# Loading the weights of two modes at a time: doubled places and doubled loads from mode 17 to mode 46 of a spectral-mix kernel

## Chip, cores, metric

One core of one Trainium2 chip. The metric is the device time of one execution in microseconds (us); the medians are over repeated runs. The span of a profile is a little shorter than the device time (424.8 us against 426.6 us for the kernel before), as it runs from the first to the last instruction of the program. An execution in which the core's clock is held lower would be set apart as slow.

## The reference

A sliding-window causal attention over 8 batches, 8 heads, 576 positions of 64 channels gives x of shape 8 x 576 x 512. Then follows a spectral mix, which is where the change lies:

```python
X = np.fft.rfft(x, axis=1)                       # along the sequence
Xr, Xi = np.real(X[:, :64]), np.imag(X[:, :64])  # 64 modes are kept
Yr = einsum('bmd,mde->bme', Xr, w_r) - einsum('bmd,mde->bme', Xi, w_i)
Yi = einsum('bmd,mde->bme', Xr, w_i) + einsum('bmd,mde->bme', Xi, w_r)
...                                              # inverse transform, y
u = x + y
return u + np.maximum(u @ w_ch, 0.0)
```

Each of the 64 modes has its own 512 x 512 matrices w_r and w_i in fp32, 1 MiB each. Mode 0 needs only w_r, so 127 matrices are read, each once: 133 MB of the 162.5 MB that the kernel reads. The arithmetic per matrix is small (8 batches), so this is a kernel that streams weights.

## The kernel before

It has three phases: attention (to about 147 us), the modes (to 390 us), and a tail that turns the modes back and writes the output. Weights are narrowed from fp32 to bf16 by the DMA, which only GpSimd (POOL) issues here, and start in the attention phase. Every load fills one place of 512 KB:

```python
def load_w(i, pool, tag, wt=None):
    m, im = divmod(i + (i > 0), 2)             # mode, real or imaginary
    if wt is None:
        wt = pool.tile([128, NC, DM], BF16, name="wt", tag=tag)
    src = moe_w_i if im else moe_w_r
    nc.gpsimd.dma_start(out=wt, in_=src[m].rearrange("(p c) e -> p c e", c=NC))
    wtiles[m, im] = wt
```

33 loads (modes 0 to 16) go out during the attention phase. From then on a place is refilled as soon as its mode has been used. There are 13 such places: LW = 5 that last to the end ("wl") and MW = 8 that are later needed for other data ("wm", which may hold no mode from 48, 50, 52 or 54 on). One more and then three more are opened late.

```python
def refill_w(m, im):                           # after the matmuls of (m, im)
    nonlocal nw
    i = max(2 * m - 1 + im, 0)
    if i in slot_of:
        free.append(slot_of.pop(i))
    if im or not m:
        free.extend(opens.pop(m, []))
    while nw < NLOAD and free:
        kind, j, last = slot = free.pop(0)
        if mode_of(nw) >= last:
            continue
        ...                                    # load_w into that place
        slot_of[nw] = slot
        nw += 1
```

A mode is eight matmuls on TensorE (PE), four on w_r and four on w_i, with other work between the modes. In the cuts of code, three dots mark what is left out, and the comments after # are mine.

The softmax here doesn't subtract the row's maximum and nothing guards it: scores larger than these inputs give would overflow.

Of the kernel before, what the change touches and what calls it, by code (L numbers as in the profile page):

```python
# [10 lines left out]
FP32R = mybir.dt.float32r  # L11
BF16 = mybir.dt.bfloat16
# [8 lines left out]
def view(ap, off, dims):  # L21

    return bass.AP(ap.tensor, ap.offset + off, [list(ap.ap[0])] + [list(d) for d in dims])
# [3 lines left out]
def kernel(  # L27
# [10 lines left out]
    nc = tc.nc  # L38
    B, H, S, D = q.shape
    NM = moe_w_r.shape[0]  # L40
    DM = moe_w_ch.shape[0]
# [4 lines left out]
    NC = DM // 128  # L46
    VW = 66
    RUN = S // 32
    LW = 5
    EW = 13  # L50
# [12 lines left out]
    keep = ctx.enter_context(tc.tile_pool(name="keep", bufs=1))  # L63
    wl = ExitStack()
    xqp = wl.enter_context(tc.tile_pool(name="xqp", bufs=1))
    wlate = wl.enter_context(tc.tile_pool(name="wlate", bufs=LW))

    ident_bf = consts.tile([128, 128], BF16, name="ident_bf")
    ident_r = consts.tile([128, 128], FP32R, name="ident_r")
    x_sb = keep.tile([128, B, NT, DM], BF16, name="x_sb")  # L70
    XQ = xqp.tile([128, NC, 3, B, NM], BF16, name="XQ")


    p1 = ExitStack()
    wearly = p1.enter_context(tc.tile_pool(name="wearly", bufs=EW, side="right"))
# [28 lines left out]
    NLOAD = 2 * NM - 1  # L104
    wtiles = {}

    def mode_of(i):
        return (i + 1) // 2

    def load_w(i, pool, tag, wt=None):  # L110
        m, im = divmod(i + (i > 0), 2)
        if wt is None:
            wt = pool.tile([128, NC, DM], BF16, name="wt", tag=tag)
        src = moe_w_i if im else moe_w_r
        nc.gpsimd.dma_start(out=wt, in_=src[m].rearrange("(p c) e -> p c e", c=NC))  # L115
        wtiles[m, im] = wt

    trigF = acons.tile([128, NT, 2 * NM], BF16, name="trigF")
    warm = acons.tile([128, 512], BF16, name="warm")
# [223 lines left out]
    def dft_turn(b):  # L343
        ps = ps_misc.tile([128, NC, 2, NM], BF16, name="pxq", tag="misc")
        for c in range(NC):
            nc.tensor.transpose(out=ps[:, c, :, :].rearrange("p r m -> p (r m)"), in_=Xs[b][:, c, :],
                                identity=ident_bf)
        nc.vector.tensor_copy(out=view(XQ, (B + b) * NM, [[3 * B * NM, NC], [B * NM, 2], [1, NM]]), in_=ps)
        nc.scalar.mul(out=view(XQ, b * NM, [[3 * B * NM, NC], [1, NM]]), in_=ps[:, :, 1, :], mul=-1.0)

    nw = 0
    EARLY = LW + EW

    def early(n):
        nonlocal nw
        for _ in range(n):
            if nw < EARLY:
                pool, tag = (wlate, "wl") if nw < LW else (wearly, "we")
                load_w(nw, pool, tag)
                nw += 1  # L360

    def spare(t):
# [28 lines left out]
    with tc.manual_schedule(engines={mybir.EngineType.PE, mybir.EngineType.Pool}):  # L391
# [49 lines left out]
        for w in range(last_unit + 1, NWIN + 1):  # L441
# [14 lines left out]
            if w in (NWIN - 4, NWIN - 1):  # L456
                i = (B - 2) % 2 if w == NWIN - 4 else (B - 1) % 2
                spare(kTs[i])
                spare(qtp.tile([128, 4, S], BF16, name="qT"))
            if w in (NWIN - 4, NWIN):  # L460
                i = (B - 2) % 2 if w == NWIN - 4 else (B - 1) % 2
                for j in range(2):
                    spare(vts[i][:, j])
                if w == NWIN - 4:
                    vt_mode = mode_of(nw - 1)
# [23 lines left out]
    YTl = late.tile([128, NC, B, R], FP32R, name="YTl")  # L489
    wch = late.tile([128, NC, DM], FP32R, name="wch")  # L490

    MW = 8
    wmid = p2.enter_context(tc.tile_pool(name="wmid", bufs=1, side="right", reuse_waits="tile"))
    mids = {j: wmid.tile([128, NC, DM], BF16, name="wt", tag=f"wm{j}") for j in range(MW)}
    late2 = p2.enter_context(tc.tile_pool(name="late2", bufs=1, side="right", reuse_waits="tile"))

    trigI = late2.tile([128, S + 128], FP32R, name="trigI")
# [7 lines left out]
    M0 = L0 * MG  # L505
# [2 lines left out]
    ML = MG - NLM  # L508
    ME = NM - NLM
    slot_of, opens = {}, {}  # L510
    for j in range(LW):
        opens.setdefault(mode_of(j), []).append(("wl", j, NM))
    for j in range(MW):
        at = mode_of(LW + (j > 1) * (EW + 1 - j)) if j else vt_mode
        opens.setdefault(at, []).append(("wm", j, M0 + 2 * (j // 2)))
    free = []

    def refill_w(m, im):

        nonlocal nw  # L520
        i = max(2 * m - 1 + im, 0)
        if i in slot_of:
            free.append(slot_of.pop(i))
        if im or not m:
            free.extend(opens.pop(m, []))
        while nw < NLOAD and free:
            kind, j, last = slot = free.pop(0)
            if mode_of(nw) >= last:
                continue
            if kind == "wl":  # L530
                load_w(nw, wlate, "wl")
            elif kind == "wx":
                load_w(nw, wx, "wx")
            elif kind == "wm":
                load_w(nw, wmid, f"wm{j}", mids.pop(j, None))
            else:
                load_w(nw, None, None, kind[:, j])
            slot_of[nw] = slot
            nw += 1

    MQ = 4
    held = []
# [20 lines left out]
    def xq(c, m, im, dims):  # L563
        return view(XQ, (c * 3 + 1 - im) * B * NM + m, dims)

# [19 lines left out]
    with ExitStack() as p2a:  # L585
# [30 lines left out]
        for m in range(L0 * MG):  # L616
            mode(m)
            if m == 1:
                for b in range(1, B, 2):
                    tc.keep_in_program_order(nc.scalar.copy(out=x_sb[64:128, b - 1, NT - 1, :],  # L620
                                                            in_=x_sb[64:128, b, NT - 1, :]))
# [75 lines left out]
                                            in0=view(trigI, 0, [[RL, NC * B], [1, RL]]), scalar1=0.0,  # L697
                                            scalar2=None, op0=ALU.mult)

    wx = wl.enter_context(tc.tile_pool(name="wx", bufs=1))  # L700
    opens.setdefault(M0, []).insert(0, ("wx", 0, NM))

    Yp = {}

    def batch_tile(b):

        if b not in Yp:
            Yp[b] = wmid.tile([128, 2, DM], FP32R, name=f"Y{b}", tag=f"wm{b}")
        return Yp[b]

    def pair_tile(what, b):

        return batch_tile(b)[:, ("yw", "Yb").index(what), :]
# [30 lines left out]
    for b in range(0, B, 2):  # L744
        whole = [(b + i, t) for i in range(2) for t in range(NT - 1)]
        at = {0: len(whole), B - 2: 0}.get(b, NT - 1)
# [33 lines left out]
    def spread(b, h):  # L780

        ps = []
        for j in range(2):
            psj = lo.tile([128, DM], FP32, name="psj", tag=f"s{j}")
            for i in range(2):
                nc.tensor.matmul(out=psj[64 * i:64 * i + 64], lhsT=view(ident_bf, j, [[2, 64]]),  # L786
                                 rhs=x_sb[:, b, 2 * h + i, :], start=True, stop=True)
            ps.append(psj)
        for j in range(2):
            evac(x_sb[:, b, 2 * h + j, :], ps[j], j)  # L790

    def spread_pair(b):

        psj = lo.tile([128, DM], FP32, name="psj", tag="s2")
        nc.tensor.matmul(out=psj, lhsT=turn, rhs=x_sb[:, b, NT - 1, :], start=True, stop=True)
        evac(x_sb[:, b, NT - 1, :], psj, b % 4 == 0)
# [5 lines left out]
    with tc.manual_schedule(engines={mybir.EngineType.PE}):  # L802
        for m in range(M0, ME):
            while len(spreads) > 5 * B // 2 * (ME - 1 - m) // (ME - M0):
                b0, h = spreads.pop(0)
                spread(b0, h) if h < 2 else spread_pair(b0)
            if (m - M0) % 2 == 0 and (m - M0) // 2 < B // 2:
                b0 = m - M0
                mode(m, lambda: spectrum(b0))
                spectrum(b0 + 1)  # L810
            else:
                mode(m)
            if m == M0 + B - 2:
                wy = late.tile([128, 3, NC, DM], BF16, name="wy", tag="yt")
                free.extend([(wy, j, NM) for j in range(3)])
                refill_w(m, 1)

        while held:
            held.pop(0)()
        NR = 2 * R + RL * (B - 2)  # L820
        YT2 = wlate.tile([128, NC, NR], FP32R, name="YT2", tag="wl")
        nc.vector.tensor_copy(out=view(YT2, 0, [[NR, NC], [R, 2], [1, R - RL]]), in_=YTl[:, :, 0:2, 0:R - RL])

        def middle_rows(b0, nb):
            psa = ps_a.tile([128, NC, 128], FP32R, name="psa", tag="psa")
            psw = ps_a.tile([128, DM], FP32, name="psw", tag="psw")
            turned(lambda e: view(YTl, (e * B + b0) * R, [[1, R * nb]]), R * nb, psa, psw)
            for i in range(nb):
                nc.vector.tensor_copy(out=pair_tile("Yb", b0 + i)[E0:],
                                      in_=psa[R * i:R * i + R].rearrange("p c e -> p (c e)"))  # L830
                nc.scalar.copy(out=pair_tile("yw", b0 + i)[E0:], in_=psw[R * i:R * i + R, :])

        psl = ps_l.tile([128, NC, RL * B], FP32, name="psl", tag="psl")

        def last(m, im):
            last_mode(m, wtiles.pop((m, im)), im, 0, NC)

        middle_rows(2, 4)
        last(ME, 0)
        lay(0)  # L840
        lay(1)
        last(ME, 1)
        middle_rows(6, 2)
        last(ME + 1, 0)
        for n in range(2, EARLY_ROWS):
            lay(n)
        idle(1, 0)
        last(ME + 1, 1)
        for m in range(ME + 2, NM):
            for im in range(2):  # L850
                idle(1, 2)
                last(m, im)
        idle(0, 2)
# [6 lines left out]
    with tc.manual_schedule(engines={mybir.EngineType.PE, mybir.EngineType.Activation, mybir.EngineType.DVE,  # L860
                                     mybir.EngineType.Pool, mybir.EngineType.SP}):
        nc.vector.tensor_copy(out=view(YT2, R - RL, [[NR, NC], [R, 2], [1, RL]]),
                              in_=view(psl, 0, [[RL * B, NC], [RL, 2], [1, RL]]))
        nc.vector.tensor_copy(out=YT2[:, :, 2 * R:], in_=psl[:, :, 2 * RL:])
        psa = ps_a.tile([128, NC, 128], FP32R, name="psa", tag="psa")
        psw = ps_a.tile([128, DM], FP32, name="psw", tag="psw")
        turned(lambda e: YT2[:, e, 0:NR], NR, psa, psw)
        lay(EARLY_ROWS)
# [98 lines left out]
```

## Time and profile before

| kernel before | |
|---|---|
| device time, first three runs | 426.64 us (426.53 to 426.81) |
| span of the profile | 424.8 us |
| PE busy | 360.5 us, 85% |
| POOL busy | 89.5 us, 21% |
| queue 0 (POOL's loads) | 81.80 MB written |
| last weight landed | 390.0 us |
| tail after it | 34.8 us |

The prediction below shows the strip of slices, the chain, POOL's timeline and the stretches. Four more lines help to read the case. The first is a group of instructions: line, engine, operation, tile, count, then busy time and mean ns of one, then the idle time ahead of it and what ended it. The second is a row of the table of loads (count, KB written, median us from issue to landing). The last two are from the table of waits (total us, times, longest us).

```profile
L115 POOL DMA_DIRECT2D wt<-in_moe_w_r_dram x54 | 28.9, 536 | 92.2 <-DMA wt<-in_moe_w_r_dram 39.9
...
wt<-in_moe_w_r_dram POOLq DMA_DIRECT2D x54, 512.0 KB, 19.1
```

```profile
PE psy L575 <- DMA wt<-in_moe_w_i_dram: 15.5, 15, 2.2
...
PE psy L575 <- DMA wt<-in_moe_w_r_dram: 14.2, 16, 1.5
```

POOL mostly waits; a load needs 19.1 us though one ends every 2.46 us; and PE waits for weights 31 times, 29.7 us in all and 2.2 us at most.

### The profile page before, as it was taken

To read this page: it belongs to the slowest core of one execution; us is meant where nothing else is said; L and a number is where in the kernel's file an instruction comes from. 1 tells how busy PE (TensorE), PEld (TensorE's weight loads), DVE (VectorE), ACT (ScalarE), POOL (GpSimd) and SP (SyncE) were. 2 spreads that over 40 slices of the span, in tenths; PEclk is the share of its full clock that TensorE was granted. 3 is DMA by queue.
4 is the path that set the end of the run, shared out by engine and by line. 5 is a ranking of instruction groups with operands and counts; after the bars stand their busy time and mean duration, and the time that the engine had idled before them with its cause. 6 is when DMAs were issued, how large, how long until landed. Compare 5 with 4: busy or idle time off the path is not lost.

```text
span 424.8 us, 8859 instructions
## 1 busy us (share of the span) xinstructions
PE 360.5 (85%) x3762; PEld 219.2 (52%) x3772; DVE 184.7 (43%) x397; ACT 171.4 (40%) x314; POOL 89.5 (21%) x171
## 2 busy tenths in 40 slices
PE   6989998998998899467698979999859886589993
PEld 5755765665665465222265646555334443256682
DVE  5566766766764201404542422333113432140994
ACT  4585765866863311201132313122113332130993
POOL 7231231331021141221221121121211032200000
PEclk9999999999995699965799998999999999999998
DMA  8999999999999999999999999999999999994598
GB/s 144 212 213 212 213 213 212 213 213 213 213 214 213 215 213 261 213 214 213 214 213 214 213 214 214 213 215 212 214 213 213 214 213 215 213 214 95 195 384 329
DMA packets 28646, 91.98 MB, mean 217 GB/s; under 512 B 2832, under 2 KB 3088, under 8 KB 28608
## 3 DMA queue, kind: packets, MB, share of 16 engines
q0 software_dynamic: 25344, 81.80, 96.6%
q1 hardware_dynamic: 3120, 9.50, 5.8%
q8 instruction: 29, 0.48, 0.4%
q10 hardware_dynamic: 144, 0.13, 0.1%
q14 instruction: 9, 0.07, 0.0%
HBM read 162.53 MB, written 9.44 MB: 405 GB/s over the span
## 4 chain that ended last, share of the span: by engine, by line
DMA 45%; PE 40%; DVE 8%; issue 2%; ACT 2%; POOL 1%; DVEq 0%; POOLq 0%
DMA wt<-in_moe_w_r_dram 32%; DMA wt<-in_moe_w_i_dram 9%; PE pso L316 7%; PE psy L575 7%; PE pst L218 6%; DMA wy<-in_moe_w_i_dram 5%; PE pso L885 4%; PE psv L235 3%; DVE x_sb L324 3%; PE psx L338 3%; PE pss L371 3%; PE pss L272 2%; PE pss L291 2%; DVE vT L59 2%; PE psw L724 1%
## 5 line engine op out<-in xcount | busy, mean ns | idle before, releaser
L575 PE MATMUL psy<-wt,XQ 128*32 128x512 bf16 (+1 forms) x404 | 96.6, 409 | 30.8 <-DMA wt<-in_moe_w_i_dram 15.5
L575 PEld LDWEIGHTS <-XQ 128*32 128x32 bf16 x476 | 48.6, 131 | 76.5 <-issue 57.0
L604 DVE CAST xT<-pxt 128x256 fp32r<-128x256 bf16 (+1 forms) x68 | 26.3, 434 | 53.8 <-PE pxt L597 34.1
L115 POOL DMA_DIRECT2D wt<-in_moe_w_r_dram x54 | 28.9, 536 | 92.2 <-DMA wt<-in_moe_w_r_dram 39.9
L611 ACT CAST Z<-psz 128x512 fp32r<-128x512 f32 x36 | 21.1, 586 | 66.6 <-PE psz L609 66.5
L115 POOL DMA_DIRECT2D wt<-in_moe_w_i_dram x52 | 28.0, 539 | 82.0 <-DMA wt<-in_moe_w_i_dram 43.7
L297 ACT ACTIVATE et<-pss 128x512 bf16<-128x512 f32 x72 | 39.2, 600 | 13.5 <-PE pss L291 13.4
L609 PE MATMUL psz<-wch,xT 128*128 128x512 f32 x144 | 42.4, 432 | 0.9 <-DVE xT L604 0.9
L316 PE MATMUL pso<-vt,et 128*64 128x65 bf16 (+1 forms) x576 | 34.3, 210 | 4.8 <-DVE x_sb L324 4.7
L609 PEld LDWEIGHTS psz<-wch,xT 128*128 128x128 f32 x144 | 27.1, 200 | 15.0 <-issue 8.7
L316 PEld LDWEIGHTS <-et 128*64 128x64 bf16 (+1 forms) x576 | 24.0, 114 | 17.1 <-issue 9.6
L59 DVE COPY x_sb<-psy 128x256 f32<-128x256 f32 x15 | 6.4, 424 | 56.7 <-PE psy L575 56.7
L324 DVE TENSOR_TENSOR x_sb<-pso,rcp 128x640 bf16<-128x640 f32 x32 | 26.3, 823 | 0.9
L58 ACT COPY x_sb<-psy 128x256 f32<-128x256 f32 x15 | 5.6, 373 | 50.2 <-DVE x_sb L59 50.2
L885 PE MATMUL pso<-Y,trigI 128*128 128x512 f32 x80 | 23.1, 402 | 0.1
L908 DVE TENSOR_TENSOR ot<-pso,x_sb 128x512 f32<-128x512 f32 x35 | 22.2, 685 | 1.5 <-PE pso L885 1.1
L272 PE MATMUL pss<-band,ident_bf 64*64 64x512 bf16 x136 | 20.6, 414 | 1.5 <-ACT et L297 1.5
L59 DVE CAST x_sb<-psj 128x512 bf16<-128x512 f32 x18 | 12.2, 688 | 21.3 <-PE psj L786 18.3
L59 DVE COPY vT<-pst 128x768 bf16<-128x768 bf16 x16 | 15.3, 958 | 13.0 <-PE pst L218 13.0
L890 ACT ACTIVATE pso<-pso 128x512 f32<-128x512 f32 x36 | 19.2, 597 | 0.0
L58 ACT CAST x_sb<-psj 128x512 bf16<-128x512 f32 x18 | 10.5, 585 | 19.6 <-PE psj L786 19.6
L291 PE MATMUL pss<-qT,kT 64*64 64x128 bf16 (+1 forms) x640 | 17.3, 221 | 0.3 <-issue 0.3
(157 smaller groups left out, 501.3 us busy)
## 6 DMA issues: line engine op xcount, KB each, us to landing
wt<-in_moe_w_r_dram POOLq DMA_DIRECT2D x54, 512.0 KB, 19.1
wt<-in_moe_w_i_dram POOLq DMA_DIRECT2D x52, 512.0 KB, 19.1
out_dram<-ot SPq DMA_DIRECT2D x15, 512.0 KB, 4.2
rk<-in_k_dram POOLq DMA_DIRECT2D x8, 576.0 KB, 9.7
rq<-in_q_dram POOLq DMA_DIRECT2D x8, 576.0 KB, 13.6
rv<-in_v_dram POOLq DMA_DIRECT2D x8, 576.0 KB, 12.3
wy<-in_moe_w_r_dram POOLq DMA_DIRECT2D x3, 512.0 KB, 17.7
wy<-in_moe_w_i_dram POOLq DMA_DIRECT2D x3, 512.0 KB, 19.1
```

The source lines that it names most:

```text
L59: return nc.vector.tensor_copy(out=o, in_=i)
L115: nc.gpsimd.dma_start(out=wt, in_=src[m].rearrange("(p c) e -> p c e", c=NC))
L218: nc.tensor.transpose(out=ps[64 * hh:64 * hh + 64, c, :], in_=src[:, hh, (c0 + c) * D:(c0 + c + 1) * D], identity=ident_bf)
L272: nc.tensor.matmul(out=pss[(2 * w + hh) % 3][64 * half:64 * half + 64, :], lhsT=ident_bf[pp, pp], rhs=view(band[pp], 128 * half, [[0, WIN ...
L291: nc.tensor.matmul(out=pss[(2 * w + hh) % 3][64 * half:64 * half + 64, col:col + nq], lhsT=kTs[b % 2][pp, g, 64 * kb:64 * kb + 64], rhs=qT ...
L297: nc.scalar.activation(out=et[:, hh, :], in_=pss[(2 * w + hh) % 3], func=ACT_F.Exp, scale=EX_SCALE)
L316: nc.tensor.matmul(out=pso[po, hh, (i // 2) * VW:(i // 2) * VW + D + 1], lhsT=et[pk, hh, col:col + 64], rhs=vt[pk, 1 - f % 2, 2 * hh + g / ...
L324: nc.vector.tensor_tensor(out=view(x_sb, b * NT * DM + g * D, [[4 * D, 2], [DM, NT], [1, D]]), in0=view(pso, 0, [[512, 2], [VW, NT], [1, D]]),
L575: nc.tensor.matmul(out=psy[r0:r0 + k, :], lhsT=xq(c, m, im, [[NM, k]]), rhs=w[:, c, :], start=(im + c == 0), stop=(im == (m > 0) and c == ...
L604: nc.vector.tensor_copy(out=xT[:, :, w * k:w * k + w], in_=view(psts[k], j, [[128, NC], [n, w]] if n > 1 else [[128, NC], [1, 64], [64, 2]]))
L609: nc.tensor.matmul(out=psz, lhsT=xT[:, c, :], rhs=wch[:, c, :], start=(c == 0), stop=(c == NC - 1))
L885: nc.tensor.matmul(out=tps[n], lhsT=trigI[:, tr:tr + 128], rhs=pair_tile(what, bb), start=False, stop=stop and r0 + k == 128, skip_group_c ...
```

## The change

The intent is to have fewer, larger DMAs: from mode 17 to mode 46 one load brings the same half (real or imaginary) of two neighbouring modes, 2 MiB read and 1 MiB written, into a double place. For the last modes, 47 to 63, a double place is split in two single ones, so that the last weights come one by one. The core of the diff:

```diff
+    WP = [wlate.tile([128, 2, NC, DM], BF16, name="wt", tag=f"wp{j}") for j in range(LW // 2)]
+    W1 = wlate.tile([128, NC, DM], BF16, name="wt", tag="w1")
...
+    def load_two(m, im, wt):
+        src = moe_w_i if im else moe_w_r
+        nc.gpsimd.dma_start(out=wt, in_=src[m:m + 2].rearrange("m (p c) e -> p m c e", c=NC))
+        for j in range(2):
+            wtiles[m + j, im] = wt[:, j]
...
-    MW = 8
+    MW = 4
-    mids = {j: wmid.tile([128, NC, DM], BF16, name="wt", tag=f"wm{j}") for j in range(MW)}
+    mids = [wmid.tile([128, 2, NC, DM], BF16, name="wt", tag=f"wm{j}") for j in range(MW)]
...
+    M2, M1 = mode_of(nw), M0 - 1                # 17 and 47
+    items = [(m, im, True) for m in range(M2, M1, 2) for im in range(2)]
+    items += [(m, im, False) for m in range(M1, NM) for im in range(2)]
...
+            fit = [s for s in free if (s[1] or not two) and s[2] > m1 + two]
+            if not fit:
+                break
...
+            if two:
+                load_two(m1, im1, wt)
+                slot_of[m1 + 1, im1] = slot      # free only after the second mode
+                continue
+            if pair:
+                free.insert(at, (wt[:, 1], False, last))
+                slot = (wt[:, 0], False, last)
```

The rest of the diff fits the early loads, the tail and the places opened late to the doubled tiles; the memory is the same. (The comments after # are not in the diff.)

More of the change, by code (lines that the diff above doesn't have):

```diff
@@ L65 @@
     xqp = wl.enter_context(tc.tile_pool(name="xqp", bufs=1))
-    wlate = wl.enter_context(tc.tile_pool(name="wlate", bufs=LW))
+    wlate = wl.enter_context(tc.tile_pool(name="wlate", bufs=1))
     ident_bf = consts.tile([128, 128], BF16, name="ident_bf")
@@ L357, in early @@
             if nw < EARLY:
-                pool, tag = (wlate, "wl") if nw < LW else (wearly, "we")
-                load_w(nw, pool, tag)
+                if nw < LW:
+                    load_w(nw, None, None, WP[nw // 2][:, nw % 2] if nw < LW - 1 else W1)
+                else:
+                    load_w(nw, wearly, "we")
                 nw += 1
@@ L510 @@
     slot_of, opens = {}, {}
-    for j in range(LW):
-        opens.setdefault(mode_of(j), []).append(("wl", j, NM))
-    for j in range(MW):
-        at = mode_of(LW + (j > 1) * (EW + 1 - j)) if j else vt_mode
-        opens.setdefault(at, []).append(("wm", j, M0 + 2 * (j // 2)))
+    M2, M1 = mode_of(nw), M0 - 1
+    assert nw == 2 * M2 - 1
+    items = [(m, im, True) for m in range(M2, M1, 2) for im in range(2)]
+    items += [(m, im, False) for m in range(M1, NM) for im in range(2)]
+    for j, wt in enumerate(WP):
+        opens.setdefault(mode_of(2 * j + 1), []).append((wt, True, NM))
+    opens.setdefault(mode_of(LW - 1), []).append((W1, False, ME - 3))
+    for j, wt in enumerate(mids):
+        at = mode_of(LW + EW + 1 - 2 * j) if j else vt_mode
+        opens.setdefault(at, []).append((wt, True, M0 + 2 * j))
     free = []
     def refill_w(m, im):
-        nonlocal nw
-        i = max(2 * m - 1 + im, 0)
-        if i in slot_of:
-            free.append(slot_of.pop(i))
+        if (m, im) in slot_of:
+            free.append(slot_of.pop((m, im)))
         if im or not m:
             free.extend(opens.pop(m, []))
-        while nw < NLOAD and free:
-            kind, j, last = slot = free.pop(0)
-            if mode_of(nw) >= last:
-                continue
-            if kind == "wl":
-                load_w(nw, wlate, "wl")
-            elif kind == "wx":
-                load_w(nw, wx, "wx")
-            elif kind == "wm":
-                load_w(nw, wmid, f"wm{j}", mids.pop(j, None))
-            else:
-                load_w(nw, None, None, kind[:, j])
-            slot_of[nw] = slot
-            nw += 1
+        while items:
+            m1, im1, two = items[0]
+            fit = [s for s in free if (s[1] or not two) and s[2] > m1 + two]
+            if not fit:
+                break
+            wt, pair, last = slot = fit[0]
+            at = free.index(slot)
+            free.pop(at)
+            items.pop(0)
+            if two:
+                load_two(m1, im1, wt)
+                slot_of[m1 + 1, im1] = slot
+                continue
+            if pair:
+                free.insert(at, (wt[:, 1], False, last))
+                slot = (wt[:, 0], False, last)
+            load_w(2 * m1 - 1 + im1, None, None, slot[0])
+            slot_of[m1, im1] = slot
     MQ = 4
@@ L698 @@
                                             scalar2=None, op0=ALU.mult)
-    wx = wl.enter_context(tc.tile_pool(name="wx", bufs=1))
-    opens.setdefault(M0, []).insert(0, ("wx", 0, NM))
+    wx = wl.enter_context(tc.tile_pool(name="wx", bufs=1)).tile([128, NC, DM], BF16, name="wt")
+    opens.setdefault(M0, []).insert(0, (wx, False, NM))
     Yp = {}
     def batch_tile(b):
-        if b not in Yp:
-            Yp[b] = wmid.tile([128, 2, DM], FP32R, name=f"Y{b}", tag=f"wm{b}")
-        return Yp[b]
+        p = b // 2
+        if p not in Yp:
+            Yp[p] = wmid.tile([128, 2, 2, DM], FP32R, name=f"Y{p}", tag=f"wm{p}")
+        return Yp[p][:, b % 2]
     def pair_tile(what, b):
@@ L814 @@
                 wy = late.tile([128, 3, NC, DM], BF16, name="wy", tag="yt")
-                free.extend([(wy, j, NM) for j in range(3)])
+                free.extend([(wy[:, j], False, NM) for j in range(3)])
                 refill_w(m, 1)
@@ L820 @@
         NR = 2 * R + RL * (B - 2)
-        YT2 = wlate.tile([128, NC, NR], FP32R, name="YT2", tag="wl")
+        YT2 = wlate.tile([128, NC, NR], FP32R, name="YT2", tag="w1")
         nc.vector.tensor_copy(out=view(YT2, 0, [[NR, NC], [R, 2], [1, R - RL]]), in_=YTl[:, :, 0:2, 0:R - RL])
```

## The prediction

> **What bounds the kernel now.** I first read the strip of 40 slices and the table of DMA queues, because the diff touches loads alone.
>
> ```profile
> PE   6989998998998899467698979999859886589993
> PEclk9999999999995699965799998999999999999998
> DMA  8999999999999999999999999999999999994598
> GB/s 144 212 213 212 213 213 212 213 213 213 213 214 213 215 213 261 213 214 213 214 213 214 213 214 214 213 215 212 214 213 213 214 213 215 213 214 95 195 384 329
> q0 software_dynamic: 25344, 81.80, 96.6%
> ```
>
> The DMA row is full from the second slice to the 36th, that is to about 382 us, at 213 GB/s whatever else runs, while TensorE (PE) falls to 4 to 7 tenths in several slices. The bytes are those written as bf16; fp32 is read, so 213 written is 426 read. (The slice with 261 holds the one load that is not narrowed.) Then I read the chain of work that ended last: its last stretch before the tail is nothing but weight loads.
>
> ```profile
> 273.98 20.46 DMA wt<-in_moe_w_r_dram
> ...
> 294.98 18.83 DMA wt<-in_moe_w_r_dram
> ...
> 370.83 19.17 DMA wy<-in_moe_w_i_dram
> ```
>
> The last weight (mode 63, imaginary) lands at 370.83 + 19.17 = 390.0 us (the packets end near 387; the landing is told some 2 to 3 us later), and 424.8 - 390.0 = 34.8 us of tail follow. Third, GpSimd's (POOL) timeline, which shows how loads are paced:
>
> ```profile
> 70.82 0.70 POOL L97 DMA_DIRECT2D rk<-in_k_dram  x1 [8.92 <-PE pst L218]
> ...
> 190.33 0.53 POOL L115 DMA_DIRECT2D wt<-in_moe_w_r_dram  x1 [1.89 <-DMA wt<-in_moe_w_r_dram]
> 192.78 0.53 POOL L115 DMA_DIRECT2D wt<-in_moe_w_i_dram  x1 [1.92 <-DMA wt<-in_moe_w_i_dram]
> 195.24 0.53 POOL L115 DMA_DIRECT2D wt<-in_moe_w_r_dram  x1 [1.93 <-DMA wt<-in_moe_w_r_dram]
> ```
>
> An issue takes 0.53 us and comes every 2.46 us; between them POOL waits for the landing of an earlier load. The median weight load lands 19.1 us after its issue, and 19.1 / 2.46 = 7.8: eight loads are in flight, and the ninth waits for the first. So POOL is a valve behind a full queue, not the limit. Landing times in the trace agree: from load 39 (mode 20 real, 175.11 us) to load 86 (mode 43 imaginary, 290.62) the step is 115.51 / 47 = 2.458 us, without a hole. Last, the busy time in stretches (columns: length, PE, PE weight load, DVE, ACT, POOL, clock, DMA share, GB/s):
>
> ```profile
> 170.80:293.00 122.20, 102.09 (x486) 55.95 (x486) 40.99 (x138) 26.56 (x56) 26.95 (x53) 0.89 1.06 213
> 293.00:352.00 59.00, 47.85 (x235) 24.35 (x236) 16.70 (x29) 15.74 (x31) 12.70 (x24) 1.00 1.06 213
> 352.00:390.05 38.05, 27.74 (x245) 15.39 (x241) 9.62 (x17) 7.55 (x15) 4.22 (x8) 0.96 0.98 197
> ```
>
> A mode needs two loads, 4.92 us of DMA. The first stretch holds 122.2 / 4.92 = 24.8 modes, so PE is busy 102.09 / 24.8 = 4.1 us per mode. PE has about 16% to spare there, 19% in the second stretch, 27% in the third: it follows the loads.
>
> **What the Trainium skill says.** "DMA: Bandwidth & Descriptors", section Anatomy of one DMA, gives a DMA about 2.0 us of fixed cost plus its bytes over 436 GB/s, mostly completion latency, and its section Measured advises at least 1 MiB per DMA. That is what makes the change look good. But the trace disagrees with reading this as a price in throughput: 1 MiB read per 2.458 us is 427 GB/s, so with eight in flight the 2 us are hidden. The section Where 436 GB/s comes from puts the ports' ceiling at 435.2 GB/s, at which 1 MiB takes 2.409 us; the trace comes within 2% of that. The section The descriptor swizzle says that a 128-partition load gives each of 16 engines 8 data pairs and one completion. The queue table agrees exactly: 127 weight loads x (128 + 16) + 24 loads of q, k and v x (256 + 16) + one of 512 + 16 make 18288 + 6528 + 528 = 25344, the number printed. Fourth, "TensorE: Matmul & The Clock Gate", Part 1, has the clock halve after an idle window of some 3.4 us. The clock row agrees: 0.5 to 0.7 in the 18th to 20th slices (181 to 212 us), where PE is 6 to 7 tenths busy.
>
> **The change part by part.** 15 spare places are filled before the modes start, so 18 + 15 = 33 loads cover modes 0 to 16. Modes 17 to 46 were 60 single loads and become 30 of two modes. Modes 47 to 63 stay 34 single loads.
>
> *Removed on POOL:* 60 x 0.53 = 31.8 us. *Added:* a double has 256 rows, as has a load of k, which took 0.70 us to issue: 30 x 0.70 = 21 us. POOL falls from 89.5 to about 79 us busy. It was not the bound: worth 0.
>
> *Removed on the DMA engines:* 30 completions on each of 16 engines. How much can that be? Load time above the skill's ceiling is 2.458 - 2.409 = 0.049 us; if it were all per load, the gain would be 30 x 0.049 = 1.5 us. But in the first part weights alternate with loads of q, k and v: the first five such pairs took (61.65 - 35.42) / 5 = 5.246 us by their landings. At the ceiling a pair takes 2.409 x (1 + 576/512) = 5.119, so the surplus is 0.127 us for two completions and 8 + 16 = 24 data packets per engine. With 8b + a = 0.049 and 24b + 2a = 0.127, b is 0.0036 per packet and a is 0.020 per completion. Estimate: 30 x 0.02 = **0.6 us saved**, with 0 and 1.5 as ends. Data packets and bytes stay the same (the second mode lies 1 MiB on in memory, so the reads cannot merge).
>
> *Moved:* the first half of a pair lands later. A double takes 4.92 us; the order is both real parts, then both imaginary parts, so mode 17's second half arrives with mode 18's. PE then gets two modes' work at once (8.2 us) every 9.83 us, instead of 4.1 every 4.92. This changes when PE waits, not the end of a pair.
>
> *Places:* 13 single places were in turn (5 + 8); now 6 doubles hold 12, and the odd one can take only a single load. A double place is free only once its second mode has read it. So at the landing of a pair's last double the other 4 doubles, 19.7 us, are still queued; the real part comes free after about one mode's work (4.1 us), leaving some 15.5 us queued. At the start the doubles open at modes 1, 2, 7, 8, 9 and 14. Mode 7 ended at 155.8 us, when what is queued reaches 165.2, and the first reuse, after mode 18's real part at 169 to 173 us, finds work to 187. The thinnest place is mode 54: four halves, the odd place and one more are 6 places, one or two of them held by PE, so 4 x 2.46 = 9.8 us are queued; before it was also six. POOL needs 0.7 us and a load some 2 us to start. **The DMA queue never runs dry**, so nothing is added on the path.
>
> *Tail:* modes 47 to 63 are loaded singly, so the last weight is used as soon after its landing as now; 34.8 us stay. Sum: 426.64 - 0.6 + 0 = 426.0; as some landings show hiccups of about a microsecond (3.8 us for the load that landed at 294.45), I round to **426.2 us**.
>
> **The rivals.** *A, the fixed cost is real.* If 2 us, or a good part, were saved on each of 30 loads, the time would be far lower; 0.3 us each would give 9 us, 417 us and faster by 2%. Against it: the steady step of 2.458 us, which leaves 0.049 to save. I give this 2%. *B, coarse places starve the queue.* PE comes in bursts; between them it idles some 2 us or more, the clock drops, its work grows towards twice, the places come free too late and DMA gets holes. For it: the clock already falls to 0.5 to 0.7 from 181 to 212 us, and PE at its worst reads a weight 7.2 us after its landing (mode 33 real). Against it: 15.5 us are queued at the moment of a refill, and a PE that lags is busy, so its clock rises. If it happened, a few holes of 1 to 3 us would give 429 to 434 us; over 435 would take 9 us of holes. *C, false waits or slower reads.* If a half of a split place waited for its other half, each mode from 47 on would wait one load longer, and the tail would grow by one load, 2.5 us, to 429. Against it: the three places in one tile that serve modes 58 to 63 are loaded and read separately already, and PE read them within 0.5 us of landing. Reads at two spots 1 MiB apart could be slower; no trace shows it. If by 1%, 30 x 4.92 x 0.01 = 1.5 us.
>
> **Range and chances.** The core is 425.1 to 426.7, from the ends of the completion's cost. Hiccups and a small hole widen it upwards: 424.7 to 428.4. Faster by over 2% (below 418) 0.02, slower by over 2% (above 435) 0.04, within 0.94.
>
> **What would show each step right or wrong.** Right: queue 0 has 25344 - 30 x 16 = 24864 packets; the strip stays at 9 and 213 GB/s up to the 36th slice; doubles land every 4.90 to 4.92 us; the last weight lands within 1.5 us of 390.0, and 34.8 us follow. POOL's busy time falls by about 10 us and its waits for landings shrink with no effect. PE's waits for weights get fewer and longer. Wrong: a slice of 170 to 310 us under 205 GB/s (rival B), doubles landing in under 4.85 us (A) or over 4.95 (C), or PE reading a weight of modes 60 to 63 over 1 us after it landed.

## The result, and the profile after

| | before | after |
|---|---|---|
| device time, median of 6 runs each | 426.72 us (426.53 to 426.81) | 426.01 us (425.92 to 427.18) |
| ratio | | 0.999 (0.9977 to 1.0003) |
| the same again, with more rounds (run after_again) | 426.81 us, 11 runs | 425.99 us, 6 runs (425.78 to 426.31) |
| ratio | | 0.9958 (0.9925 to 0.9991) |

A ratio is the mean time of one kernel's fast runs over that of the other's fast runs in the same rounds, so it is not quite the ratio of the medians. In the second row the kernel before had four runs of 428.6 to 430.1 us among its eleven; they count as fast, they lift its mean, and nothing here explains them. I therefore lean on the medians, which agree in both rows: 0.7 and 0.8 us less, a sixth of a per cent.

The strip of slices and the load queue of the kernel after (the row DMA is digit for digit that of before):

```profile
PE   6999999999988897363698977977569997588993
PEclk9999999999996899556599999999968999999998
GB/s 142 212 213 212 212 216 211 214 213 211 215 213 214 215 212 261 214 216 212 215 216 213 215 215 214 215 214 213 216 213 214 214 213 214 213 214 96 194 387 329
q0 software_dynamic: 24864, 81.80, 96.6%
```

The stream is as full as before up to the 36th slice: no slice from the second on is under 211 GB/s until it ends. In seven of the 13 slices from 170 to 308 us, where doubles run, it reads 215 or 216; before, in one. The queue has 480 packets fewer, 30 x 16, with the same bytes. POOL's timeline, and the rows of its loads (count, KB, us to landing):

```profile
227.88 0.71 POOL L122 DMA_DIRECT2D wt<-in_moe_w_r_dram  x1 [4.93 <-PE psy L592]
228.74 0.71 POOL L122 DMA_DIRECT2D wt<-in_moe_w_i_dram  x1
...
247.46 0.71 POOL L122 DMA_DIRECT2D wt<-in_moe_w_r_dram  x1 [2.89 <-PE psy L592]
248.32 0.71 POOL L122 DMA_DIRECT2D wt<-in_moe_w_i_dram  x1
```

```profile
wt<-in_moe_w_r_dram POOLq DMA_DIRECT2D x15, 1024.0 KB, 23.0
wt<-in_moe_w_i_dram POOLq DMA_DIRECT2D x15, 1024.0 KB, 25.4
wt<-in_moe_w_r_dram POOLq DMA_DIRECT2D x25, 512.0 KB, 16.9
```

Where doubles run, what releases POOL has changed from the landing of an earlier load to PE, that is to a place being read out. So POOL's gate is there the number of places and no longer eight loads in flight. POOL's busy time fell from 89.5 to 78.9 us. The waits of PE for weights, and the stretch in which doubles run:

```profile
PE psy L592 <- DMA wt<-in_moe_w_i_dram: 25.6, 14, 3.8
...
PE psy L592 <- DMA wt<-in_moe_w_r_dram: 15.9, 11, 5.0
```

```profile
170.80:293.00 122.20, 91.98 (x491) 54.00 (x491) 40.98 (x138) 26.52 (x56) 18.40 (x27) 0.85 1.06 214
```

PE waits 25 times in place of 31, but 41.5 us in place of 29.7. It loses nothing by that: its busy time in this stretch fell from 102.1 to 92.0 us, although its clock fell from 0.89 to 0.85, and it was never what the end waited for. The end of the chain:

```profile
371.13 18.30 DMA wt<-in_moe_w_i_dram
389.43 0.05 issue
389.48 0.64 PE psl L793 x16
```

The last weight lands at 371.13 + 18.30 = 389.43 us, 0.57 us earlier than before, and 424.3 - 389.4 = 34.9 us of tail follow, as before. So the whole gain is in the stream. Where in the stream, the landing records of the trace say (own table of landings, us):

```
                           before                     after
both halves of mode 20     177.54                     177.52
both halves of mode 46     306.40                     305.94  (0.46 earlier)
mode 63, imaginary         390.00                     389.43  (0.57 earlier)
one mode's half, steady    115.51 / 47 = 2.458        doubles: 107.66 / 22 = 4.894
```

(The doubles are those that landed from 177.52 to 285.18 us.) Two single loads take 4.915 us, one double 4.894: **0.022 us saved per double**. Thirty of them are 0.65 us, and that accounts for the result within its scatter: 0.11 us of the 0.57 came after mode 46, where nothing was changed, and in the second trace of this kernel (after_again) mode 46 came 0.75 us earlier than before and the last weight 0.76.

### The profile page after: what moved, and what is told of

Read it like the earlier page. It is cut to its first block, busy times and chain, and to the rows that moved or that the text cites. A ratio compares the mean times of both kernels' runs of the same rounds, so it can differ in the third digit from the quotient of the medians.

```text
span 424.3 us, 8788 instructions
## 1 busy us (share of the span) xinstructions
PE 348.0 (82%) x3772; PEld 215.7 (51%) x3772; DVE 184.5 (43%) x397; ACT 171.2 (40%) x314; POOL 78.9 (19%) x141
## 3 DMA queue, kind: packets, MB, share of 16 engines
q0 software_dynamic: 24864, 81.80, 96.6%
## 4 chain that ended last, share of the span: by engine, by line
PE 38%; DMA 37%; issue 12%; DVE 8%; POOL 2%; ACT 2%; POOLq 0%; DVEq 0%
DMA wt<-in_moe_w_r_dram 23%; DMA wt<-in_moe_w_i_dram 14%; PE pso L324 7%; PE pst L226 6%; PE psy L592 4%; PE pso L903 4%; PE psv L243 3%; DVE x_sb L332 3%; PE psw L742 3%; PE pss L280 2%; PE pss L381 2%; PE psx L346 2%; PE pss L299 2%; DVE vT L59 2%; POOL wt L122 1%
## 5 line engine op out<-in xcount | busy, mean ns | idle before, releaser
L592 PE MATMUL psy<-wt,XQ 128*32 128x512 bf16 (+1 forms) x404 | 86.1, 427 | 42.6 <-DMA wt<-in_moe_w_i_dram 25.6
L592 PEld LDWEIGHTS <-XQ 128*32 128x32 bf16 (+1 forms) x476 | 46.2, 132 | 82.7 <-issue 65.8
L626 PE MATMUL psz<-wch,xT 128*128 128x512 f32 x144 | 40.3, 417 | 0.4 <-DVE xT L621 0.4
L626 PEld LDWEIGHTS psz<-wch,xT 128*128 128x128 f32 x144 | 26.1, 193 | 11.6 <-issue 5.7
L122 POOL DMA_DIRECT2D wt<-in_moe_w_r_dram x15 | 10.7, 713 | 77.7 <-PE psy L592 68.7
L117 POOL DMA_DIRECT2D wt<-in_moe_w_r_dram x25 | 13.6, 544 | 37.9 <-PE psy L592 22.8
L59 DVE CAST x_sb<-psj 128x512 bf16<-128x512 f32 x18 | 12.2, 688 | 18.5 <-PE psj L804 15.6
L122 POOL DMA_DIRECT2D wt<-in_moe_w_i_dram x15 | 10.7, 714 | 36.1 <-PE psy L592 35.1
```

What stands on the lines that cost most here:

```text
L59: return nc.vector.tensor_copy(out=o, in_=i)
L122: nc.gpsimd.dma_start(out=wt, in_=src[m:m + 2].rearrange("m (p c) e -> p m c e", c=NC))
L592: nc.tensor.matmul(out=psy[r0:r0 + k, :], lhsT=xq(c, m, im, [[NM, k]]), rhs=w[:, c, :], start=(im + c == 0), stop=(im == (m > 0) and c == ...
L626: nc.tensor.matmul(out=psz, lhsT=xT[:, c, :], rhs=wch[:, c, :], start=(c == 0), stop=(c == NC - 1))
```

## Experiments

Eight kernels ran. The first four ask what a load costs beside its bytes, the other four how far the queue is from running dry.

**after_again**: the changed kernel, unedited, five rounds.

> The changed kernel once more, for a tighter interval. Theory (the bound is the DMA stream; what a double saves is one completion, 0.020 us by the estimate of the prediction): 0.5 to 0.7 us less than before, 426.0 to 426.2. Rival (noise, nothing was saved): the interval of the ratio holds 1.000, and the doubles land 4.916 us apart, twice the 2.458 of single loads.

Measured: 425.99 us against 426.81. In its trace the doubles that landed from 177.38 to 285.03 us were 107.65 / 22 = 4.893 us apart. The interval of the ratio, 0.9925 to 0.9991, leaves out 1.000, though the odd runs of the kernel before help in that; the step of 4.893 instead of 4.915 does not depend on them, and four_doubles, below, has it a third time (107.64 / 22 = 4.893 us). The rival of mere noise falls.

**two_loads**: the double places without the double loads.

```diff
-        nc.gpsimd.dma_start(out=wt, in_=src[m:m + 2].rearrange("m (p c) e -> p m c e", c=NC))
         for j in range(2):
+            nc.gpsimd.dma_start(out=wt[:, j], in_=src[m + j].rearrange("(p c) e -> p c e", c=NC))
             wtiles[m + j, im] = wt[:, j]
```

> The changed kernel with its double places, but each place filled by two loads of one mode: the places alone, without the merging. Theory: the gain is in the merged loads, so it goes: about 426.6, 0.6 above the changed kernel; queue 0 has 25344 packets again. Rival (the places or the order of the loads bring the gain): it stays at 426.0.

Measured: 426.76 us (426.58 to 427.79), against 426.81 before and 425.99 for the changed kernel in the same rounds; the last weight landed at 390.06 us, and single loads are again 2.458 us apart (44 of them from 177.62 to 285.76 us). The queue has its packets back:

```profile
q0 software_dynamic: 25344, 81.80, 96.6%
```

The places and the changed order of the loads give and cost nothing that these runs show. The gain is in the merged loads.

**half_loads** and **short_rows** are edits of the kernel before, in which the 94 loads from mode 17 on are made worse. The first cuts each load in two loads of half rows:

```diff
-        nc.gpsimd.dma_start(out=wt, in_=src[m].rearrange("(p c) e -> p c e", c=NC))
+        rows_ = src[m].rearrange("(p c) e -> p c e", c=NC)
+        if m < 17:
+            nc.gpsimd.dma_start(out=wt, in_=rows_)
+        else:
+            for c in range(0, NC, 2):
+                nc.gpsimd.dma_start(out=wt[:, c:c + 2], in_=rows_[:, c:c + 2])
```

> The kernel before with each of the 94 weight loads from mode 17 on cut into two loads of half rows: 8 more data packets and 1 more completion per engine and load. With b = 0.0036 per packet and a = 0.020 per completion: 94 x (0.029 + 0.020) = 4.6 us more, 431.3. Rival A of the prediction (a good part of 2 us per load is really paid in throughput, say 0.3): 28 us more, 455.

The second leaves one load but cuts its rows into shorter packets (the last line of the edit becomes `nc.gpsimd.dma_start(out=wt, in_=rows_, max_dma_last_dim=2 * DM)`):

> The kernel before with the same 94 loads left whole, but their rows cut in two packets: 8 more data packets, no more completions. With b = 0.0036: 94 x 0.029 = 2.7 us more, 429.4, and so 1.9 us less than the half loads. If the surplus over the ceiling were all per completion: 0 more, 426.7. If all per packet (0.006): 4.6 more, as the half loads.

Measured: half_loads 432.76 us (431.52 to 434.26), +6.0; short_rows 445.27 us (445.13 to 445.5), +18.5. The second is far off what was expected, and the packet count of short_rows says why: my edit did not do what I meant.

```profile
GB/s 147 212 214 211 214 212 213 212 213 215 214 213 213 208 209 234 197 197 197 198 198 198 198 198 198 197 197 198 197 197 198 197 198 198 197 198 121 155 383 334
DMA packets 112870, 91.98 MB, mean 207 GB/s; under 512 B 2832, under 2 KB 99344, under 8 KB 112832
```

Before, 3088 packets were under 2 KB; now there are 99344 - 3088 = 96256 = 94 x 1024 more. The rows were cut in eight packets of 512 B and not in two of 2 KB: each engine has 64 data packets per load and not 16. That makes the run a better measure of the price of a packet than the one I had planned. The last weight landed at 408.45 us, 18.45 later than before; 18.45 / 94 = 0.196 us per load for 56 packets more, **0.0035 us per packet**. The prediction had b = 0.0036, from two rows of landings in the attention phase. The forecast of 2.7 us for 8 packets becomes, for 56, 94 x 56 x 0.0036 = 19 us. Both other readings that I had written down fall: that all of the surplus is per completion (0) and, scaled in the same way, that all of it is per packet (0.006 x 56 x 94 = 32 us).

In half_loads, from the load that landed at 206.04 us to the one at 297.50, 73 half loads took 91.46 us, which is 2.506 us per whole load in place of 2.458: 0.048 for 8 packets and one completion, where 0.049 was expected. Taking 8 x 0.0035 off leaves **0.020 us per completion**, which the doubles confirm from the other side with 0.022. (No edit here changes completions without loads, so "per completion" stands for all that comes once per load. The trace's packet records give a completion 22 ns on its engine, which fits; but the eight data packets of a load add up to 8 x 0.324 = 2.59 us there, more than the step of 2.458, so the records overlap and do not prove it.) Over 94 loads 0.048 gives 4.5 us; the run lost 6.0. The rest, some 1.5 us, I put down to holes in the stream; the profiled execution was the slowest of the six (434.26 us) and shows more of them, as its last weight landed at 397.94 us, 7.9 later than before. One is plain: POOL stood still from 187.98 to 190.48 us, and the load issued then landed 2.81 us after its forerunner in place of 1.25. Eight half loads in flight are only half the bytes, 9.7 us from issue to landing; the stream has less to live on when POOL is late. What POOL waited for there the profile does not tell, and it stays open. Rival A (a real price of 0.3 us or more per load, 455 us) is out.

**four_doubles** and **three_doubles**: the changed kernel with two, or three, of the four middle double places never opened, so that four or three of six remain.

```diff
     for j, wt in enumerate(mids):
+        if j < 2:          # three_doubles: j < 3
+            continue
         at = mode_of(LW + EW + 1 - 2 * j) if j else vt_mode
```

> The changed kernel without two of its six double places (the middle ones 0 and 1 are never opened): 8 half places. Theory (the queue has slack): when a pair's second double lands, two doubles (9.8 us) are still queued; both places are free some 1 to 3 us later and a new load needs about 3 us, so the stream holds: 0 to 1 us more than the changed kernel, 426 to 427. Rival B (coarse places starve the queue): holes already here, 429 to 436.

> The changed kernel with three double places (6 half places; the middle ones 0, 1 and 2 are never opened). Theory: one double (4.9 us) is queued when a pair's second double lands, the next is issued 1 to 3 us later and needs some 3 us to start, so small holes come whenever TensorE is late: 3 to 20 us more than the changed kernel, holes between 170 and 300 us, none after. If it stays at 426, the cushion of the changed kernel is far larger than I thought.

**six_singles**: the kernel before with six of its 13 places, the memory of three_doubles (`for j in range(7, MW):` when the middle places are opened).

> The kernel before with 6 single places in place of 13 (the middle ones 0 to 6 are never opened): the same memory as the three doubles. Theory: TensorE holds one or two, four are queued (9.8 us), so the stream holds: 426.5 to 428. The difference to the three doubles is the price of coarse places. Rival (the number of bytes in turn counts, not their grain): as the three doubles.

Measured: four_doubles 426.29 us (425.95 to 428.03), three_doubles 433.07 (429.73 to 434.17), six_singles 427.76 (426.97 to 428.55), before 426.69 in the same rounds. With four doubles the last weight landed at 389.23 us, earlier than before: a third of the double places can go at no cost that these runs show (the changed kernel itself did not run in the same rounds). With three, the stream has holes, and POOL's timeline shows each place being issued just when a read frees it:

```profile
GB/s 142 211 213 213 213 215 212 213 212 213 214 214 211 214 214 234 214 198 213 214 211 186 212 193 215 195 212 202 213 213 214 213 213 214 214 214 124 189 386 321
```

```profile
225.35 0.71 POOL L122 DMA_DIRECT2D wt<-in_moe_w_r_dram  x1 [2.55 <-PE psy L594]
233.40 0.71 POOL L122 DMA_DIRECT2D wt<-in_moe_w_i_dram  x1 [7.33 <-PE psy L594]
```

The load issued at 225.35 us landed at 235.42, and the one issued at 233.40 at 242.58: 7.16 us apart in place of 4.89. Slices of 186 to 202 GB/s lie between 180 and 300 us and none after; the last weight landed at 395.32 us, 6.1 us later than in after_again (389.24). This is rival B, and it needs half the memory taken away. It did not come by the falling clock, which rival B put into its chain: from 150 to 310 us the clock was 0.93, against 0.88 in the changed kernel. Coarse places do have a price: with the same memory in single places the loss against the kernel before was 1.1 us and not 6.4.

**late_split**: the changed kernel with doubles up to mode 56 (`M1 = M0 + 9` in place of `M0 - 1`).

> The changed kernel with doubles up to mode 56 in place of 46. Theory: the doubles end where the middle places end; from mode 53 only two double places are left, so modes 55 and 56 are loaded into places just read, with an empty queue: holes of 3 to 6 us around 335 to 350 us, 430 to 434. Rival (the split serves only the last weights of the tail): no change, 425.8 to 426.2, as ten more completions are saved.

Measured: 441.86 us (440.85 to 442.36), 15.2 us more than before. The direction was right and the size was not. The strip, then POOL's timeline:

```profile
GB/s 144 212 214 212 212 214 207 185 214 213 214 206 200 214 214 260 214 214 214 214 214 214 215 214 214 214 214 214 215 214 141 191 26 214 214 214 148 166 386 324
```

```profile
340.00 0.70 POOL L122 DMA_DIRECT2D wt<-in_moe_w_r_dram  x1 [13.73 <-PE psy L592]
342.78 0.72 POOL L122 DMA_DIRECT2D wt<-in_moe_w_i_dram  x1 [2.08 <-PE psy L592]
359.59 0.72 POOL L122 DMA_DIRECT2D wt<-in_moe_w_r_dram  x1 [16.10 <-PE psy L592]
```

There are two holes, in the 31st to 33rd slices: the load issued at 340.00 landed at 347.76, 9.01 us after its forerunner (4.1 too late), and the one issued at 359.59 at 367.34, 14.65 us after its forerunner (9.8 too late). Together they are 13.9 us of the 15.9 by which the last weight, at 405.10 us, was later than in after_again (389.24). (The other 2 us were lost in the attention phase, where nothing was changed: the load before the first double landed at 157.37 us, against 155.23.) I had expected holes of 3 to 6 us, and for the second I had left out that a place is free only after the *second* mode's read: the pair of modes 53 and 54 landed at 352.69 us, and only then could both modes run, with PE's other work between them, 6.9 us until the next issue. Add 7.75 us from an issue to the landing when nothing is queued, take off the 4.9 that a double takes anyway, and 9.8 us remain. So the split at mode 47 is needed because only two double places outlive the middle ones, and not for the tail alone.

I saw in these runs no version that would beat both kernels by more than the 0.02 us of each further merged load, so none was tried.

## Why the prediction was right

The time forecast was 426.2 us in a range of 424.7 to 428.4, and 0.94 for "within 2%"; 426.01 and 425.99 were measured.

- *The DMA stream is the bound, POOL is only a valve.* Shown: POOL lost 10.6 us of busy time (about 10 forecast) and its waits changed their cause, and the time followed the landing of the last weight: 0.57 us earlier, 0.5 to 0.7 us less in span and time.
- *0.6 us saved by 30 completions, from a = 0.020 and b = 0.0036.* Shown three ways: doubles 4.894 us apart (4.90 to 4.92 forecast, so a hair below), 0.048 us per load in half_loads, 0.0035 us per packet in short_rows; and the 24864 packets are exact. With two_loads, which has the doubled places but not the doubled loads, the gain is gone. That the forecast came so near was in part luck. The pairs' step of 5.246 us, on which a and b rest, lies between 5.234 and 5.274 in the ten traces, though nothing differs there; by the same sums these ends would have given an a of 0.032 and of -0.008. And a also takes over any error of the skill's ceiling of 435.2 GB/s. The runs of this document do not need that ceiling.
- *Nothing added on the path because the queue never runs dry.* Shown by the strip, and by four_doubles. But one term of the working was mis-sized. "the real part comes free after about one mode's work (4.1 us), leaving some 15.5 us queued" holds for the worst case only: the least that was queued at a double's issue after a read was 15.9 us (the issue at 220.39 us, with the queue filled to 236.26). Usually it was more, as PE runs the second mode's real part soon after the pair is complete. The pair of modes 29 and 30 was complete at 226.44 us, the place was refilled at 227.88, 1.4 us later, and 246.01 - 227.88 = 18.1 us were then queued. "The thinnest place is mode 54 ... 9.8 us" was a little too rosy: the thinnest moment there was the issue at 350.07 us with the queue filled to 357.52, 7.5 us.
- *Bursts move PE's waits and not the end.* Shown: fewer and longer waits, 41.5 us for 29.7. The clock did fall, as rival B had it (0.85 for 0.89), but PE had the time.
- *Rival A* is out by half_loads. *Rival B* is real, but at three double places and not at six. *Rival C*: reads from two spots 1 MiB apart cost nothing (4.894 us is less than twice a single load). The half places of the last modes caused no false wait either. The two parts of mode 59 share one double place (by the rule of refilling, gone through by hand); the real part landed at 367.34 us and its matmuls began at 367.38, while the imaginary part landed at 369.77. Mode 63, in the same place, went alike (387.00 and 387.05, the other part at 389.43), and the tail is unchanged.
- *Readings and signs that were wrong, without harm to the forecast.* The landing is not told 2 to 3 us after the last packets: a load comes in 16 shares, those of the last weight landed between 385.27 and 390.00 us in the kernel before, and its last packet ended at 389.67. The strip falls early, as some shares are done first. Two passages on the clock are cut from the prediction. One said that the trace agrees with the skill on the idle time after which the clock halves. It does not: the clock of the kernel before fell at 179.2 us to 0.50, and from PE's first matmul to then its longest idle gap was 2.16 us, shorter than that time. The other said that the clock of a busy PE rises; from 128.0 to 145.1 us it was 0.50 while PE was busy for 15.4 of 17.1 us. And one sign of being wrong came up: mode 60's real part was read 2.0 us after its landing (372.24 and 374.27 us). It was badly chosen, as in the kernel before that delay was 3.1 us (372.78 and 375.89).

## What to carry to other kernels

When a queue of loads is always full, the latency of a load is hidden and merging loads saves only what each load takes from the stream beside its data packets, here 0.02 us of 2.46; look at the step between landings, not at the time from issue to landing, to see what there is to gain. Merged loads pay for that in grain: their places come free later and in pairs, so first count what is queued at the moment when a place comes free, down to the last places that remain. A side measurement of two mixtures of loads (here weights with and without q, k and v between them) can split a surplus of 2% into its parts, here well enough to forecast a change of a sixth of a per cent; but look at the scatter of the mixture's step first, which in ten traces was wide enough to spoil it.

## What the Trainium skill lacked or had wrong

- "DMA: Bandwidth & Descriptors", Anatomy of one DMA: the fixed cost of about 2.0 us is right as a latency. In late_split a double issued at 340.00 us into an empty queue landed after 7.76 us; less 0.70 for the issue and 4.89 for the transfer, 2.2 us remain. The page calls the semaphore write itself essentially free, and lacks a figure for what is left as a price in throughput when loads are queued: 0.020 to 0.022 us per load here.
- The same page, Measured, and its rule of at least 1 MiB per DMA for 75% of peak: with eight loads in flight, single loads of 1 MiB read reached 1 MiB / 2.458 us = 427 GB/s, 98% of the ceiling of 435.2, and half loads of half the size still 1 MiB / 2.506 us = 418. The rule does not say how many loads are in flight.
- The same page, Where 436 GB/s comes from, says without a condition that HBM at about 358 GB/s binds a load to SBUF. Its section Measured limits that to two cores streaming at once, and this program, on one core, bears the limit out: it read at 427 GB/s for over 200 us.
- The same page, Why small descriptors are slow, gives about 3 cycles per packet and no time. At the 850 MHz that the page has for the fabric, that is an estimate of 3.5 ns (the section does not name the clock), and short_rows shows 3.5 ns, so the two agree.
- No page read has it: the core's own instruction fetches appear to delay weight loads. In the traces of before, after, after_again and two_loads, 15 loads landed 0.5 us or more later than the usual step after 30 us, by 0.6 to 1.7 us, and each of them 2.0 to 3.3 us after the start of a 16 KB packet of the queue "instruction" (0.9 to 1.1 us long): the load that landed at 294.45 us in the kernel before, for one, follows a packet at 292.4. But such packets are frequent, and only 15 of 104 were followed by a late load. No experiment was made, so this is a coincidence in time and not a shown cause.
